# Exchanging two transpose copies between ScalarE and VectorE, and copying x out earlier, in the opening of a linear-attention + SwiGLU kernel

## Chip, cores, metric

One core of a Trainium2 chip. The metric is the device time of one execution in microseconds; lower is better. Most comparisons below use several executions of each kernel, taken in turn on the same chip. The four groups of experiments ran on four chips (0, 7, 6 and 9), so a kernel is compared with the kernel before of its own rounds; sums over all rounds mix chips.

## The reference, cut to what matters

For each of 8 batches and 8 heads, 576 tokens of 64 dimensions: softmax of the queries along the head dimension, softmax of the keys along the tokens, `kv = k^T v`, `x = q kv`. Then a SwiGLU block over all 4608 tokens (512 wide, 1536 hidden).

```python
q_s = exp(q - max) / sum          # along the 64 dimensions of a head
k_s = exp(k - max) / sum          # along the tokens
kv  = einsum('bhsd,bhse->bhde', k_s, v)
x   = einsum('bhsd,bhde->bhse', q_s, kv)   # -> [4608, 512]
out = (silu(x @ w_gate) * (x @ w_val)) @ w_out
```

Inputs and output are fp32; the kernel computes in bf16 with fp32 sums.

## The kernel before: the parts concerned

Heads come in two groups of four (group 0 and 1). A group's normalised queries `qs` are transposed on TensorE into PSUM (`tp`) in two pieces, of 5 and 4 token blocks (640 and 512 columns), and copied to SBUF as `qt`. `kv` is scaled into `kn`, and `x = kn^T qt` is copied into `xt`, which the gate and value products read. Only batch 0 has this opening; later batches hide behind the SwiGLU products.

```python
spin(8)                    # warm-up products on zeros
spin(6, first)             # ... from the first row sum of batch 0's queries on
key_sum(0)
turn_pe(0, 0, 0)           # transposes, group 0, piece of 640 and piece of 512
turn_pe(0, 0, 1)
turn_out(0, 0, 0, nc.scalar)     # copy PSUM -> SBUF
exp_of("k", 0, 1)
turn_out(0, 0, 1, nc.scalar)
norm_mul(0, 1, BANKS)
spin(6)
kv_first(0)                # the first kv product
key_sum(1)
scale_first(0, nc.scalar)  # kn of group 0, both halves on ScalarE
turn_pe(0, 1, 0)
turn_pe(0, 1, 1)
turn_out(0, 1, 0, nc.vector)
turn_out(0, 1, 1, nc.vector)
xp0 = x_mm(0, 0, 0), x_mm(0, 0, 1)      # the first x product
kv_first(1, *BANKS[0])     # the second kv product, values in two pieces
kv_first(1, *BANKS[1])
x_out(0, 0, 0, xp0[0], (nc.scalar, None))
scale_first(1, nc.vector)  # kn of group 1: half on ScalarE, half on VectorE
x_out(0, 0, 0, xp0[0], (None, nc.vector))
x_out(0, 0, 1, xp0[1])
xp1 = x_mm(0, 1, 0), x_mm(0, 1, 1)      # the second x product
...
for m in range(MT):
    m_unit(0, S, m, by_group=(m == 0))  # the gate and value products start
```

A later part turns out to matter, the preparation of batch 1 some 28 us further on:

```python
exp_of("q", 1, 0)
exp_of("q", 1, 1)
norm_sum(1, 0)
norm_mul(1, 0)             # VectorE, bf16, 128x1152
norm_sum(1, 1)
...
i = norm_mul(1, 1)
cast_v(1, 0)               # GpSimd: batch 1's values, fp32 -> bf16
c = cast_v(1, 1)
tc.add_manual_dep(c.ins, i.ins.name, SYNC, reason="order of the vector port")
```

The second cast is made to wait for the second normalisation; the first cast waits only for its data.

The softmax here doesn't subtract the row's maximum and nothing guards it: scores larger than these inputs give would overflow.

Of the kernel before, what the change touches and what calls it, by code (L numbers as in the profile page):

```python
# [15 lines left out]
def kernel(  # L16
# [10 lines left out]
    nc = tc.nc  # L27
# [19 lines left out]
    def bank(name):  # L47
        return psp.tile([128, 512], FP32, tag="ps", name=name)
# [57 lines left out]
    def copy(eng, out, in_):  # L106
        if eng is nc.scalar:
            nc.scalar.copy(out=out, in_=in_)  # L108
        else:
            eng.tensor_copy(out=out, in_=in_)  # L110
# [5 lines left out]
    def exp_of(what, b, G, pieces=((0, T),)):  # L116
        s = st.setdefault((b, G), {})
        e = s["e" + what] = at.tile([128, T, 2, 64], BF16, tag="e" + what, name="e" + what)
        src = raw[what, b, G].rearrange("p h (t d) -> p t h d", d=64)
        for t0, t1 in pieces:  # L120
            nc.scalar.activation(out=e[:, t0:t1], in_=src[:, t0:t1], func=AF.Exp)  # L121
# [21 lines left out]
    def norm_mul(b, G, pieces=((0, T),), engs=None):  # L143
        s = st[b, G]
        eq2 = s["eq"].rearrange("p t h d -> p (t h) d")
        qs = s["qs"] = at.tile([128, T, 128], BF16, tag="qs", name="qs")
        for (t0, t1), eng in zip(pieces, engs or (nc.vector, nc.vector)):
            n = 2 * (t1 - t0)
            last = eng.tensor_mul(  # L149
                qs[:, t0:t1, :].rearrange("p t (h d) -> p (t h) d", d=64),  # L150
                eq2[:, 2 * t0:2 * t1, :],
                s["rr"][:, 2 * t0:2 * t1].to_broadcast([128, n, 64]),
            )
        return last

    def turn_pe(b, G, i):
        s = st[b, G]
        if i == 0:
            s["qt"] = at.tile([128, T, 128], BF16, tag="qt", name="qt")
        t0, t1 = BANKS[i]  # L160
        tp = s["tp", i] = psp.tile([128, 1024], BF16, tag="ps", name="tp")
        for t in range(t0, t1):
            j = t - t0
            nc.tensor.transpose(  # L164
                out=tp[:, j * 128:(j + 1) * 128], in_=s["qs"][:, t, :], identity=ident
            )

    def turn_out(b, G, i, eng):
        s = st[b, G]
        t0, t1 = BANKS[i]  # L170
        copy(
            eng,
            s["qt"][:, t0:t1, :],
            s["tp", i][:, 0:(t1 - t0) * 128].rearrange("p (t c) -> p t c", c=128),
        )
# [19 lines left out]
    def x_mm(b, G, i):  # L195
        s = st[b, G]
        t0, t1 = BANKS[i]
        xp = [bank("xp") for _ in range(2)]
        for g in range(2):
            for h in range(2):  # L200
                r = slice(64 * h, 64 * h + 64)
                nc.tensor.matmul(  # L202
                    out=xp[h][64 * g:64 * g + 64, 0:64 * (t1 - t0)],
                    lhsT=s["kn"][r, g, :],
                    rhs=s["qt"][r, t0:t1, 64 * g:64 * g + 64],
                    start=True, stop=True,
                )
        return xp

    def x_out(b, G, i, xp, engs=(nc.scalar, nc.vector)):  # L210
        t0, t1 = BANKS[i]
        n = 64 * (t1 - t0)
        c0 = b * S + 64 * t0
        for h in (h for h in range(2) if engs[h] is not None):
            copy(engs[h], xt[:, 2 * G + h, c0:c0 + n], xp[h][:, 0:n])
# [137 lines left out]
    with tc.manual_schedule():  # L353
# [31 lines left out]
        def spin(n, after=None):  # L385
            idle = bank("idle")
            for _ in range(n):
                i = nc.tensor.matmul(out=idle, lhsT=zero[:, 0:128], rhs=zero, start=True, stop=True)  # L388
                if after is not None:
                    tc.add_manual_dep(i.ins, after.ins.name, SYNC, reason="start of the warm-up")  # L390
                    after = None
# [12 lines left out]
        def kv_first(G, t0=0, t1=T):  # L404
            s = st[0, G]
            if t0 == 0:
                s["kv"] = [bank("kv") for _ in range(2)]
            for t in range(t0, t1):
                for g in range(2):
                    for h in range(2):  # L410
                        nc.tensor.matmul(  # L411
                            out=s["kv"][g][HALF[h], 0:64], lhsT=s["ek"][HALF[g], t, h, :],
                            rhs=v16[G][HALF[g], h, 64 * t:64 * t + 64],
                            start=(t == 0), stop=(t == T - 1),
                        )

        def scale_first(G, eng1):
            s = st[0, G]
            kn = s["kn"] = at.tile([128, 2, 64], BF16, tag="kn1", name="kn1")
            nc.scalar.mul(kn[:, 0, :], s["kv"][0][:, 0:64], s["kvr"][:, 0:1])  # L420
            if eng1 is nc.scalar:
                nc.scalar.mul(kn[:, 1, :], s["kv"][1][:, 0:64], s["kvr"][:, 1:2])
            else:
                nc.vector.tensor_scalar_mul(kn[:, 1, :], s["kv"][1][:, 0:64], s["kvr"][:, 1:2])
# [5 lines left out]
        turn_pe(0, 0, 1)  # L430
        turn_out(0, 0, 0, nc.scalar)
        exp_of("k", 0, 1)
        turn_out(0, 0, 1, nc.scalar)
        norm_mul(0, 1, BANKS)
        spin(6)
        kv_first(0)
        key_sum(1)
        scale_first(0, nc.scalar)
        turn_pe(0, 1, 0)
        turn_pe(0, 1, 1)  # L440
        turn_out(0, 1, 0, nc.vector)
        turn_out(0, 1, 1, nc.vector)
        xp0 = x_mm(0, 0, 0), x_mm(0, 0, 1)
        kv_first(1, *BANKS[0])
        kv_first(1, *BANKS[1])
        x_out(0, 0, 0, xp0[0], (nc.scalar, None))
        scale_first(1, nc.vector)
        x_out(0, 0, 0, xp0[0], (None, nc.vector))
        x_out(0, 0, 1, xp0[1])
        xp1 = x_mm(0, 1, 0), x_mm(0, 1, 1)  # L450
        x_out(0, 1, 0, xp1[0])
# [153 lines left out]
```

## Time and profile before

| what | us |
|---|---|
| three runs | 311.02, 311.06, 311.29 |
| span of the profiled run | 309.7 (time 311.57) |
| first gate product starts | 14.22 |
| the second x product waits for the scaled kv | 0.42 |

The span is that of the profile, from first to last instruction; the time is 1.8 us longer. The prediction below shows the chain of the opening and the timeline of ScalarE and VectorE (in brackets idle time and what ended it). One more view was not read closely before predicting and is needed later: TensorE's own timeline from the beginning (start us, duration us, engine, line, instruction, count; in brackets idle time and what ended it).

```profile
1.22 3.60 PE L388 MATMUL idle<-zero 128*128 128x512 bf16 x8 [1.22 <-DVE sel L367]
6.23 2.74 PE L388 MATMUL idle<-zero 128*128 128x512 bf16 x6 [1.41 <-DVE rs L135]
9.97 1.56 PE L388 MATMUL idle<-zero 128*128 128x512 bf16 x6
11.46 0.48 PE L411 MATMUL kv<-v,ek 64*64 64x64 bf16 x36
```

The second batch of six warm-up products takes 2.74 us, the third, of six as well, 1.56 us. TensorE's clock stepped up meanwhile: the products start 0.43 us apart in the second batch and 0.22 us apart from 10.29 us on, and in the trace's record the clock is full from 10.2 us on, early in the third.

### The profile page before, as it was taken

To read this page: it belongs to the slowest core of one execution; us is meant where nothing else is said; L and a number is where in the kernel's file an instruction comes from. 1 tells how busy PE (TensorE), PEld (TensorE's weight loads), DVE (VectorE), ACT (ScalarE), POOL (GpSimd) and SP (SyncE) were. 2 spreads that over 40 slices of the span, in tenths; PEclk is the share of its full clock that TensorE was granted. 3 is DMA by queue.
4 is the path that set the end of the run, shared out by engine and by line. 5 is a ranking of instruction groups with operands and counts; after the bars stand their busy time and mean duration, and the time that the engine had idled before them with its cause. 6 is when DMAs were issued, how large, how long until landed. Compare 5 with 4: busy or idle time off the path is not lost.

```text
span 309.7 us, 5467 instructions
## 1 busy us (share of the span) xinstructions
PE 302.8 (98%) x2182; PEld 150.3 (49%) x2182; DVE 161.9 (52%) x286; ACT 146.3 (47%) x214; POOL 32.8 (11%) x39
## 2 busy tenths in 40 slices
PE   6999999999999999999999999999999999999995
PEld 2688745554445444454445444544444444444443
DVE  3844477945754566365826492639353324433421
ACT  5843578785674375547464737455043113312300
POOL 2960021510200110002000200000000000000000
PEclk9999999999999999999999999999999999999999
DMA  7999999999347815590739352605310302020133
GB/s 273 189 195 207 275 389 389 349 219 389 79 87 200 327 33 114 135 382 13 144 74 353 102 121 61 186 0 107 72 35 0 70 11 56 3 68 8 26 71 103
DMA packets 43018, 45.78 MB, mean 148 GB/s; under 512 B 19568, under 2 KB 28272, under 8 KB 42992
## 3 DMA queue, kind: packets, MB, share of 16 engines
q1 hardware_dynamic: 34096, 39.95, 43.4%
q0 software_dynamic: 8752, 5.31, 12.0%
q8 instruction: 17, 0.28, 0.4%
q10 hardware_dynamic: 144, 0.16, 0.2%
q14 instruction: 9, 0.07, 0.1%
HBM read 37.75 MB, written 9.44 MB: 152 GB/s over the span
## 4 chain that ended last, share of the span: by engine, by line
PE 96%; DMA 1%; DVE 0%; ACT 0%; issue 0%
PE g_ps L284 30%; PE u_ps L284 30%; PE o_ps L317 29%; PE kv L189 2%; PE xp L245 1%; PE idle L388 1%; DMA q<-in_q_dram 1%; PE tp L164 1%; PE o_ps L338 1%; DVE rs L135 0%; PE xp L202 0%; PE kv L411 0%; ACT eq L121 0%; ACT xt L259 0%; PE ks L397 0%; DVE o_sb L342 0%
## 5 line engine op out<-in xcount | busy, mean ns | idle before, releaser
L291 ACT ACTIVATE sg<-g_ps 128x512 bf16<-128x512 f32 (+2 forms) x120 | 64.7, 554 | 133.6 <-PE g_ps L284 120.5
L293 DVE TENSOR_TENSOR hr<-sg,u_ps 128x512 bf16<-128x512 bf16 (+3 forms) x120 | 72.5, 616 | 86.3 <-PE u_ps L284 80.7
L284 PE MATMUL g_ps<-xt,wg 128*128 128x512 bf16 (+2 forms) x480 | 111.4, 358 | 0.1
L284 PE MATMUL u_ps<-xt,wv 128*128 128x512 bf16 (+2 forms) x480 | 111.3, 358 | 0.0
L317 PE MATMUL o_ps<-wo,hr 128*128 128x512 bf16 x420 | 93.9, 379 | 0.0
L284 PEld LDWEIGHTS <-wv 128*128 128x128 bf16 x480 | 46.9, 98 | 46.4
L284 PEld LDWEIGHTS <-wg 128*128 128x128 bf16 x480 | 46.3, 98 | 45.5 <-issue 0.6
L317 PEld LDWEIGHTS <-hr 128*128 128x128 bf16 x420 | 40.9, 98 | 48.6
L110 DVE COPY o_sb<-o_ps 128x512 f32<-128x512 f32 x33 | 22.4, 680 | 39.0 <-PE o_ps L317 39.0
L124 POOL CAST vb<-v 128x1152 bf16<-128x1152 f32 x14 | 17.8, 1277 | 135.8 <-DMA v<-in_v_dram 106.6
L135 DVE TENSOR_REDUCE rs<-eq 128x18 f32<-128x1152 bf16 (+2 forms) x18 | 21.7, 1213 | 12.7 <-ACT eq L121 12.7
L149 DVE TENSOR_TENSOR qs<-eq,rr 128x1152 bf16<-128x1152 bf16 (+2 forms) x18 | 22.1, 1234 | 0.1
L121 ACT ACTIVATE eq<-q 128x1152 bf16<-128x1152 f32 (+2 forms) x18 | 18.3, 1051 | 4.1 <-DMA q<-in_q_dram 4.0
L121 ACT ACTIVATE ek<-k 128x1152 bf16<-128x1152 f32 (+2 forms) x17 | 17.9, 1101 | 0.5 <-DMA k<-in_k_dram 0.5
L291 ACT ACT_TABLE_LOAD x12 | 15.4, 1283 | 0.2
L121 ACT ACT_TABLE_LOAD x11 | 14.1, 1283 | 0.2
L388 PE MATMUL idle<-zero 128*128 128x512 bf16 x20 | 7.9, 560 | 2.6 <-DVE rs L135 1.4
L259 ACT CAST xt<-xp 128x512 bf16<-128x512 f32 x14 | 7.8, 586 | 4.5 <-PE xp L245 4.5
L260 DVE CAST xt<-xp 128x512 bf16<-128x512 f32 x14 | 9.0, 683 | 0.7 <-PE xp L245 0.7
L189 PEld LDWEIGHTS <-ek 64*64 64x64 bf16 x504 | 6.3, 107 | 1.7 <-ACT qt L108 0.4
L189 PE MATMUL kv<-vb,ek 64*64 64x65 bf16 x504 | 6.7, 194 | 0.0
L245 PE MATMUL xp<-qt,kn 64*64 64x512 bf16 (+1 forms) x112 | 6.7, 292 | 0.0
(44 smaller groups left out, 67.4 us busy)
## 6 DMA issues: line engine op xcount, KB each, us to landing
q<-in_q_dram SPq DMA_DIRECT2D x16, 576.0 KB, 5.4
out_dram<-o_sb SPq DMA_DIRECT2D x70, 128.0 KB, 2.3
k<-in_k_dram SPq DMA_DIRECT2D x12, 576.0 KB, 7.2
v<-in_v_dram SPq DMA_DIRECT2D x12, 576.0 KB, 9.1
wo<-in_moe_w_out_dram POOLq DMA_DIRECT2D x4, 384.0 KB, 15.4
k<-in_k_dram SPq DMA_DIRECT2D x4, 320.0 KB, 8.2
k<-in_k_dram SPq DMA_DIRECT2D x4, 256.0 KB, 8.1
v<-in_v_dram SPq DMA_DIRECT2D x2, 320.0 KB, 6.9
```

The lines of the kernel that those rows point to most:

```text
L110: eng.tensor_copy(out=out, in_=in_)
L121: nc.scalar.activation(out=e[:, t0:t1], in_=src[:, t0:t1], func=AF.Exp)
L124: return nc.gpsimd.tensor_copy(out=vbs[G][:, :, :, 0:64], in_=raw["v", b, G].rearrange("p h (t d) -> p t h d", d=64),)
L135: i = nc.vector.reduce_sum(out=rs[:, 2 * t0:2 * t1], in_=eq2[:, 2 * t0:2 * t1, :], axis=mybir.AxisListType.X)
L149: last = eng.tensor_mul(qs[:, t0:t1, :].rearrange("p t (h d) -> p (t h) d", d=64), eq2[:, 2 * t0:2 * t1, :], s["rr"][:, 2 * t0:2 * t1].to_ ...
L189: nc.tensor.matmul(out=kv[g][HALF[h], c:c + 65], lhsT=ek[HALF[g], t, h, :], rhs=vbs[G][HALF[g], t, h, :], start=(t == 0), stop=(t == T - 1),)
L245: nc.tensor.matmul(out=o[h][HALF[g], c:c + 64 * (t1 - t0)], lhsT=kn[HALF[h], g, G, :], rhs=qt[G][HALF[h], t0:t1, 64 * g:64 * g + 64], star ...
L284: nc.tensor.matmul(out=gu[a][i][:, 0:w_], lhsT=(wg, wv)[a][:, kk, ms], rhs=xt[:, kk, c:c + w_], start=(kk == 0), stop=(kk == KT - 1),)
L291: nc.scalar.activation(out=sg[:, 0:w_], in_=g_ps[:, 0:w_], func=AF.Silu)
L293: nc.vector.tensor_mul(hr[:, m, r:r + w1], sg[:, 0:w1], u_ps[:, 0:w1])
L317: nc.tensor.matmul(out=o_ps, lhsT=hr[:, m, r0:r0 + 128], rhs=wo[:, m, :], start=(m == 0), stop=(m == MT - 1),)
L388: i = nc.tensor.matmul(out=idle, lhsT=zero[:, 0:128], rhs=zero, start=True, stop=True)
```

## The change

The intent: give each engine the copy that comes when it is free. ScalarE gives up group 0's second copy, which stands just ahead of its first scaling, and takes group 1's first copy from VectorE. VectorE then has room to copy x out before it scales. No instruction is added or removed.

```diff
         turn_out(0, 0, 0, nc.scalar)
         exp_of("k", 0, 1)
-        turn_out(0, 0, 1, nc.scalar)
         norm_mul(0, 1, BANKS)
+        turn_out(0, 0, 1, nc.vector)
         spin(6)
...
-        turn_out(0, 1, 0, nc.vector)
+        turn_out(0, 1, 0, nc.scalar)
         turn_out(0, 1, 1, nc.vector)
...
-        x_out(0, 0, 0, xp0[0], (nc.scalar, None))
+        x_out(0, 0, 0, xp0[0])
         scale_first(1, nc.vector)
-        x_out(0, 0, 0, xp0[0], (None, nc.vector))
         x_out(0, 0, 1, xp0[1])
```

## The prediction

> **What bounds the kernel now.** I read the page's first part, then the chain of waits that ended last, narrowed to the first 30 us, then the timeline of the two engines that the change touches, in the same stretch.
>
> The page first, for the question of which engine a saved microsecond has to reach:
>
> ```profile
> PE 302.8 (98%) x2182; PEld 150.3 (49%) x2182; DVE 161.9 (52%) x286; ACT 146.3 (47%) x214; POOL 32.8 (11%) x39
> ```
>
> TensorE is busy 98% of a span of 309.7 us. ScalarE and VectorE are about half busy, so their work counts only where TensorE stands still for it. The change sits in the opening, which ends when the first gate product starts at 14.22 us; from there TensorE runs with almost no gap. So the question is by how much that start moves. Part of the chain before it (start us, duration us, what):
>
> ```profile
> 11.53 0.41 PE kv L411 x36
> 11.94 0.31 PE ks L397 x9
> 12.25 0.52 PE tp L164 x9
> 12.77 0.37 PE xp L202 x8
> 13.14 0.36 PE kv L411 x35
> 13.49 0.02 issue
> 13.52 0.30 DVE kn L424
> 13.81 0.03 issue
> 13.84 0.45 PE xp L202 x8
> ```
>
> From 11.53 to 13.49 every piece is TensorE's own, in program order: the first kv product, the key sums, the transposes of the second group of queries, the first x product, the second kv product. Then comes the only real stop: the second kv product must be scaled into kn before the second x product can start. "Waits" puts it down as 0.42 us before that product. Only what moves this scaling, or what follows it, can move the end.
>
> What the two other engines do around it (start us, duration us, engine, line, instruction), ScalarE first:
>
> ```profile
> 9.78 0.69 ACT L108 COPY qt<-tp 128x640 bf16<-128x640 bf16 x1 [0.59 <-PE tp L164]
> 10.37 1.17 ACT L121 ACTIVATE ek<-k 128x1152 bf16<-128x1152 f32 x1
> 11.44 0.58 ACT L108 COPY qt<-tp 128x512 bf16<-128x512 bf16 x1
> 11.98 0.31 ACT L420 ACTIVATE kn<-kv,kvr 128x64 bf16<-128x64 f32 x1
> 12.20 0.31 ACT L422 ACTIVATE kn<-kv,kvr 128x64 bf16<-128x64 f32 x1
> 13.07 0.42 ACT L108 CAST xt<-xp 128x320 bf16<-128x320 f32 x1 [0.57 <-PE xp L202]
> 13.47 0.31 ACT L420 ACTIVATE kn<-kv,kvr 128x64 bf16<-128x64 f32 x1
> ...
> 12.28 0.17 DVE L402 RECIPROCAL kvr<-ks 128x2 f32<-128x2 f32 x1 [0.41 <-PE ks L397]
> 12.59 0.82 DVE L110 COPY qt<-tp 128x640 bf16<-128x640 bf16 x2
> 13.52 0.28 DVE L424 TENSOR_SCALAR kn<-kv,kvr 128x64 bf16<-128x64 f32 x1
> 13.72 1.54 DVE L110 CAST xt<-xp 128x320 bf16<-128x320 f32 x4
> ```
>
> Three things are to be seen. ScalarE is free from 12.51 to 13.07, VectorE from 11.88 (end of its last normalisation) to 12.28: both have room beside the chain. The two halves of the critical kn run at once, one per engine, 13.47 to 13.78 and 13.52 to 13.80. And VectorE's first copy of x waits until after kn, at 13.72.
>
> [...] the single records are 0.49 and 0.41 us on VectorE, 0.69 and 0.58 on ScalarE. [...] The trace has the overlap: the copy of 9.78 would end at 10.47 and the next starts at 10.37, and kn follows kn after 0.22 of its 0.31. [...] The trace shows about 0.1 us at each change between 128*128 and 64*64 (the last transpose starts at 12.55, streams about 0.05, and the first x product starts at 12.70). It stays as it is: TensorE's order is the same in both programs.
>
> **The change, part by part.** Comparing the order of instructions of the two built programs: nothing is added or removed, the tiles and sizes are the same, and three things move.
>
> (1) The 512 copy of group 0 leaves ScalarE (11.44, 0.58 us) for VectorE, where it comes right after the last normalisation: it can start near 11.80 (normalisation ends 11.88, VectorE's neighbours overlap by 0.08) and ends near 12.21. The reciprocal behind it waits for the key sums until 12.28 as before. Who gains? ScalarE's first kn at 11.98; but that needs the kv product, which ends at 11.94, so it can gain 0.03 at most. And the x product that uses it starts at 12.70 [...]; kn is out at 12.51. Gain on the path: 0.
>
> (2) The 640 copy of group 1 leaves VectorE (12.59, 0.49 us) for ScalarE. The transposes are out at 12.59 as before, and it takes 0.69. The next ScalarE instruction, the copy of x, could start at 13.07; now it starts at 12.59 + 0.69 - 0.10 = 13.17, 0.10 later. It lasts 0.42, so the critical kn on ScalarE can start at 13.17 + 0.42 - 0.10 = 13.49 to 13.50 in place of 13.47. It was waiting for the kv product then, not for ScalarE (the copy at 13.07 left the engine near 13.40). So of the 0.10 only 0.02 to 0.03 reaches the path: kn ends near 13.81, and TensorE goes on 0.05 later, at 13.86 in place of 13.84.
>
> (3) On VectorE one copy of x (320 columns) now comes before kn. The group 1 copy of 512 starts once its transposes are out, 12.77 + 0.04 = 12.81, where it started at 12.99 before. Then the copy of x starts at 12.81 + 0.41 - 0.08 = 13.14 (its data are there at 13.07) and kn at 13.14 + 0.48 - 0.08 = 13.54, in place of 13.52. Cost: 0.02, beside the 0.02 of ScalarE and not on top of it. In return the copies of x end earlier: the first at 13.62 in place of 14.20, the second near 14.16 in place of 14.53. The gate products that need them start at 14.37 and 14.62 as single records, [...] at the same pace as later groups (0.15, 0.14, 0.11 between starts against 0.14, 0.14, 0.11). So at most 0.01 us was lost there, and that is all there is to win.
>
> Sum: +0.02 at the second x product, -0.01 behind it, 0 elsewhere: between 0 and +0.03 us. [...] I put +0.04 between these.
>
> [...] the change also alters which bank a tile gets. In both programs each of the tiles from the second x product on takes a bank that is read out before TensorE gets there; from the third gate product on the order is the same with other bank numbers.
>
> **Rivals.** (a) ScalarE becomes the bound: it gets the slower copy (0.69 for 0.58 before) just ahead of the critical kn. Its idle 0.57 us before 13.07 speaks against; a transpose that is out later[...] speaks for it. It makes +0.1, at the worst +0.2: 311.2 to 311.3. (b) The swap was worth making because VectorE's copies of x came too late: the chain gives the first gate group 0.60 us against 0.49 for those after it, which looks like 0.11 us to win. Against: the single starts show no stop[...]. If it were real: -0.1, 310.95. (c) The opening gets shorter, but meets the weights: the first slice of the value weights is issued at 9.37 and such a transfer lands after a median of 5.1 us, near 14.5, and is used at 14.72. So no more than some 0.2 us could be won at all before that wait took the place of the other. (d) A shift of a few hundredths is swallowed by a later wait. TensorE does stop at 46 and 51 us for VectorE and ScalarE (0.2 and 0.3 us), but those waits hang on work that starts with TensorE's own earlier results and move along with it; I expect no swallowing, and it would make the time 311.06.
>
> **Range and chances.** 311.06 + 0.04 = 311.1 us. The three runs of before spread over 0.27 us (311.02 to 311.29), so scatter is larger than the effect: with it and the rivals from -0.1 to +0.2 I take 310.8 to 311.5. Two per cent is 6.2 us; the whole opening from 11.5 to 14.2 us is shorter than half of that, so only something unseen could do it: 0.5% for faster, 1% for slower.
>
> **What would show it.** In the changed kernel's timeline: ScalarE's kn for group 0 still at 11.98; its 640 copy at 12.59 with 0.69; its copy of x near 13.17; its critical kn at 13.50 [...]; VectorE's copy of x at 13.14 and kn at 13.54; the second x product at 13.86 and the first gate product at 14.24, within 0.1. Wrong would be: a second x product before 13.80 (I would have missed what held kn), a stop of TensorE at the first x product (12.70), or a first gate product that starts more than 0.15 us from 14.22.

Of the single records, 0.49 and 0.41 us are VectorE's copies of 640 and 512 columns, 0.69 and 0.58 us ScalarE's. A start that waited came 0.04 us after the end that it waited for (the scaling ends at 13.80, the second x product starts at 13.84). A term is cut from the sum: the terms that stand came to 0 to +0.03 us; the cut one was a possible later start of the scaling behind a copy on ScalarE, of a size that no trace here shows. The author put +0.04 us between the sum without and with it, so 311.06 + 0.04 = 311.1 us.

## The result, and the profile after

| | before | changed |
|---|---|---|
| runs of the same rounds | 311.02, 311.29, 311.06, 312.51, 311.36, 311.94 | 311.33, 311.95, 311.70, 313.17, 311.85, 312.05 |
| median | 311.33 | 311.90 |
| ratio | | 1.0015 (0.9991 to 1.0040) |

Every run whose state is on record, here and below, is recorded as "fast". When this text calls a run "slow", it means over 312.3 us, a line that is explained at the end, and "quick" means the rest. A ratio is the mean time of one kernel's fast runs over that of the other's of the same rounds, so not quite the ratio of the medians quoted. The median of 311.9 lies outside the predicted 310.8 to 311.5: either the change costs half a microsecond that the prediction did not see, or the scatter had been sized wrongly.

The profiled run of the changed kernel was one of the quick ones (311.33 us, span 309.5 us), so it cannot show where time went. It shows two things that the prediction did not expect. The first is TensorE's timeline in the opening:

```profile
1.23 3.40 PE L388 MATMUL idle<-zero 128*128 128x512 bf16 x8 [1.23 <-DVE sel L367]
6.29 1.47 PE L388 MATMUL idle<-zero 128*128 128x512 bf16 x6 [1.67 <-DVE rs L135]
8.88 1.46 PE L388 MATMUL idle<-zero 128*128 128x512 bf16 x6
10.77 0.48 PE L411 MATMUL kv<-v,ek 64*64 64x64 bf16 x36 [0.43 <-DMA v<-in_v_dram]
12.27 0.44 PE L202 MATMUL xp<-qt,kn 64*64 64x320 bf16 x8
12.53 0.46 PE L411 MATMUL kv<-v,ek 64*64 64x64 bf16 x36
13.41 0.47 PE L202 MATMUL xp<-qt,kn 64*64 64x320 bf16 x8 [0.42 <-ACT kn L420]
13.81 0.66 PE L284 MATMUL g_ps<-xt,wg 128*128 128x320 bf16 x4
```

The second batch of six warm-up products took 1.47 us here, not 2.74: the trace's record of the clock has it full from 4.3 us on, not from 10.2. This part of the program is the same in both kernels. The key sums behind it came 1.2 us earlier (7.60, not 8.77). Waits for the values and for VectorE took most of that back: the first kv product came 0.7 us earlier (10.77, not 11.46), the first gate product 0.4 us (13.81, not 14.22). From the second kv product (12.53) to the second x product (13.41) it is 0.88 us, against 12.97 and 13.84, 0.87 us, before.

The second is where half of those 0.4 us went. The waits of the stretch from 44 or 45 to 47 us (who <- for whom: total us, times, longest), before:

```profile
PEld L164 <- DVE qs L149: 0.5, 1, 0.5
```

and after:

```profile
PEld L164 <- DVE qs L149: 0.7, 1, 0.7
PE tp L164 <- DVE qs L149: 0.2, 1, 0.2
```

TensorE arrived earlier at batch 1's transposes and waited 0.2 us longer there for VectorE's normalised queries. In this trace those hang on batch 1's queries, which landed at 38.73 us, and not on TensorE. The page's chain of waits says the same in one line. Before:

```profile
PE 96%; DMA 1%; DVE 0%; ACT 0%; issue 0%
```

After:

```profile
PE 84%; DMA 8%; POOL 4%; DVE 2%; ACT 1%; issue 0%; SPq 0%
```

The chain no longer runs back to the start through TensorE. It leaves it at this wait and goes through the loads (DMA, and GpSimd, which issues the weight loads). Spans: 309.74 before, 309.49 after, so 0.25 us of the 0.42 us were left.

ScalarE's timeline of the changed kernel, to be held against the prediction's lines of before:

```profile
11.29 0.31 ACT L420 ACTIVATE kn<-kv,kvr 128x64 bf16<-128x64 f32 x1 [0.45 <-PE kv L411]
11.50 0.31 ACT L422 ACTIVATE kn<-kv,kvr 128x64 bf16<-128x64 f32 x1
11.89 0.69 ACT L108 COPY qt<-tp 128x640 bf16<-128x640 bf16 x1
12.64 0.43 ACT L108 CAST xt<-xp 128x320 bf16<-128x320 f32 x1
13.04 0.31 ACT L420 ACTIVATE kn<-kv,kvr 128x64 bf16<-128x64 f32 x1
```

Between its exponential and its first scaling ScalarE now sits idle for 0.45 us, waiting for TensorE: the freed room is not used. And in this run the 640 copy at 11.89 is out of the way before the copy of x can start, so it delays nothing.

### The profile page after: what moved, and what is told of

The parts are those of the page before. It is cut to its first block, busy times and chain, and to the rows that moved or that the text cites. A ratio compares the mean times of both kernels' runs of the same rounds, so it can differ in the third digit from the quotient of the medians.

```text
span 309.5 us, 5467 instructions
## 1 busy us (share of the span) xinstructions
PE 301.4 (97%) x2182; PEld 149.7 (48%) x2182; DVE 161.5 (52%) x286; ACT 146.5 (47%) x214; POOL 33.0 (11%) x39
## 4 chain that ended last, share of the span: by engine, by line
PE 84%; DMA 8%; POOL 4%; DVE 2%; ACT 1%; issue 0%; SPq 0%
PE o_ps L317 27%; PE g_ps L284 27%; PE u_ps L284 26%; DMA wo<-in_moe_w_out_dram 4%; DMA q<-in_q_dram 2%; PE kv L189 2%; DMA k<-in_k_dram 2%; POOL wg L96 1%; POOL wv L96 1%; PE xp L245 1%; DVE qs L149 1%; DVE rs L135 1%; PE o_ps L338 1%; POOL v L361 0%; ACT eq L121 0%; POOL v L358 0%
## 5 line engine op out<-in xcount | busy, mean ns | idle before, releaser
L121 ACT ACTIVATE eq<-q 128x1152 bf16<-128x1152 f32 (+2 forms) x18 | 18.3, 1053 | 4.2 <-DMA q<-in_q_dram 4.1
L121 ACT ACTIVATE ek<-k 128x1152 bf16<-128x1152 f32 (+2 forms) x17 | 18.0, 1103 | 0.8 <-DMA k<-in_k_dram 0.7
L388 PE MATMUL idle<-zero 128*128 128x512 bf16 x20 | 6.3, 471 | 2.9 <-DVE rs L135 1.7
```

The costliest lines, as they stand in the source:

```text
L121: nc.scalar.activation(out=e[:, t0:t1], in_=src[:, t0:t1], func=AF.Exp)
```

## The experiments

Three questions. Does the change have a cost of its own (theory B) or is it lost in scatter (theory A)? Where does the scatter come from? Can it be taken away, so that the two kernels can be compared without it?

### e1 to e4: both kernels again, and each part alone

e1 is the kernel before, unaltered; e2 the changed kernel, unaltered.

> The kernel before, unaltered, timed against itself. Theory A (the change is worth nothing that can be seen; the medians of 311.33 and 311.9 us differ by scatter from outside the program): the runs of this one kernel spread over 0.5 us or more and its ratio to itself is as far from 1 as 0.1 per cent. Theory B (the change costs a real 0.4 to 0.5 us): this kernel against itself stays within 0.05 per cent. Its trace shows which of two openings it had: full TensorE clock from about 10 us (idle products 0.43 us apart until then, first gate product at 14.2) or from about 4 us (0.22 us apart, first gate product at 13.8).

> The changed kernel again. Theory A: ratio 0.999 to 1.001, and the same two openings as the kernel before; from the last matmul of the second kv product to the second x product 0.61 us in either, as both traces so far have it. Theory B: ratio 1.0013 to 1.002, so 0.4 to 0.6 us.

e3 has the exchange of copies without the earlier copy of x (against the kernel before):

```diff
-        turn_out(0, 0, 1, nc.scalar)
         norm_mul(0, 1, BANKS)
+        turn_out(0, 0, 1, nc.vector)
-        turn_out(0, 1, 0, nc.vector)
+        turn_out(0, 1, 0, nc.scalar)
```

> The two copies of the queries exchanged, the copy of x left behind the scaling on VectorE. Theory A: ratio 0.999 to 1.001; the second x product 0.61 us after the last matmul of the second kv product. Theory B, if the exchange of copies carries the cost: ratio 1.0013 to 1.002; if the copy of x carries it: 1.000.

e4 has the earlier copy of x without the exchange:

```diff
-        x_out(0, 0, 0, xp0[0], (nc.scalar, None))
+        x_out(0, 0, 0, xp0[0])
         scale_first(1, nc.vector)
-        x_out(0, 0, 0, xp0[0], (None, nc.vector))
```

> The copy of x moved ahead of the scaling on VectorE, the copies of the queries as before. VectorE's last copy of queries ends at 13.41 in the trace of before, so the copy of x starts near 13.33, ends the engine's turn near 13.73, and the scaling starts there in place of 13.52: the second x product 0.2 us later (0.8 us after the last kv matmul). Theory A expects a ratio of 1.0003 to 1.0010 for this one, from these 0.2 us alone; theory B, if the copy of x carries the cost, 1.0013 to 1.002.

Measured, with the kernel before at 311.25 to 312.84 in 11 runs of the same rounds (mean 311.65):

| | range | mean | ratio (95%) |
|---|---|---|---|
| e1, before again | 311.25 to 312.37 | 311.59 | 0.9998 (0.9981 to 1.0016) |
| e2, changed again | 311.31 to 312.85 | 312.12 | 1.0015 (0.9997 to 1.0034) |
| e3, copies only | 311.49 to 312.55 | 311.78 | 1.0004 (0.9988 to 1.0021) |
| e4, copy of x only | 311.47 to 313.06 | 312.05 | 1.0016 (0.9996 to 1.0035) |

The kernel before spreads over 1.6 us in these rounds, six times the 0.27 us of its first three runs. But the changed kernel's mean is 0.47 us over it, as in the first rounds (0.48), so theory B was not out. The expectations are split too: the spread of e1 (1.1 us) is what theory A asked for, its ratio to itself (0.9998) what theory B asked for, and the ratios of e2 and e4 lie in theory B's range.

The traces decide what the change does on the path. e3 had the late clock step, as before, and its values in time. It is therefore the clean test of the prediction's step on ScalarE. Its ScalarE timeline:

```profile
12.59 0.69 ACT L108 COPY qt<-tp 128x640 bf16<-128x640 bf16 x1
13.18 0.43 ACT L108 CAST xt<-xp 128x320 bf16<-128x320 f32 x1
13.50 0.33 ACT L420 ACTIVATE kn<-kv,kvr 128x64 bf16<-128x64 f32 x1
```

The prediction had 12.59, 13.17 and 13.50. From the last matmul of the second kv product to the second x product it is 0.64 us in the single records of e3 and 0.61 in before and e1: the exchange costs 0.03 us, no more. In e2 and e4 the second piece of group 1's values came late and TensorE waited for it inside the second kv product. The chain of e2 in the opening (start us, duration us, what):

```profile
7.98 5.56 DMA v<-in_v_dram
13.54 0.04 issue
13.58 0.37 PE kv L411 x16
13.96 0.30 ACT kn L420
14.26 0.04 issue
14.30 0.45 PE xp L202 x8
```

So e4 could not show the 0.2 us that I expected of the copy of x alone: its kv product was held up so long that VectorE was done with the copy (at 13.51) before the scaling could start (13.68), and from kv to x it is 0.60 us. The lateness does not need the change. The transfer was issued at 8.0 us; up to about 11.4 us e2 has the same instruction order as before, and e4 up to 13.0 us, when its piece (landed at 13.24) was nearly in. And e11 below, whose opening is that of the kernel before, had the piece as late (13.21).

Then the slow runs. The profiled runs of e1 (312.37 us) and e2 (312.85 us) were slow ones, and both lost time in the same place, near 42 us, where VectorE normalises batch 1's first queries and GpSimd casts its first values. VectorE and GpSimd in that stretch, before (a quick run):

```profile
41.84 1.36 DVE L149 TENSOR_TENSOR qs<-eq,rr 128x1152 bf16<-128x1152 bf16 x1
...
42.20 2.01 POOL L124 CAST vb<-v 128x1152 bf16<-128x1152 f32 x1 [20.27 <-DMA v<-in_v_dram]
46.22 1.15 POOL L124 CAST vb<-v 128x1152 bf16<-128x1152 f32 x1 [2.01 <-DVE qs L149]
```

e2 (a slow run):

```profile
42.23 2.26 DVE L149 TENSOR_TENSOR qs<-eq,rr 128x1152 bf16<-128x1152 bf16 x1
...
42.14 1.14 POOL L124 CAST vb<-v 128x1152 bf16<-128x1152 f32 x1 [20.27 <-DMA v<-in_v_dram]
```

The same two instructions, 1.36 and 1.14 us alone, but whichever starts second is stretched: before, the cast, to 2.01; in e2, the normalisation, to 2.26. The normalisation that started at 42.23 ended at 44.49, which is 1.21 us after the cast's end at 43.28; so of its 1.36 us it had done about 0.15 in the 1.05 us beside the cast, if the rest ran at its own speed (my estimate). In e1 it is the same: the cast ran from 41.70 to 42.84, and the normalisation from 42.04 to 44.05, again 1.21 us after the cast's end. It holds in the other direction too: in the seven in which the normalisation started first, the cast ended 1.00 or 1.01 us after it, wherever it had started. The held-up casts cost nothing that can be seen (the seven traced runs that had one took 311.03 to 311.66 us). A held-up normalisation delays batch 1's transposes, for which TensorE then waits (0.6 us in e1 and e2).

The sign of it was in the page of before: the group of casts has a mean of 1277 ns in 14 instructions, while the one at 46.22 took 1.15 us. (Two more of the 14, at 55 and 59 us, were stretched too.)

### e5 to e8: the race at 42 us taken out, reversed, and a longer warm-up

e5 is the kernel before, and e6 the changed kernel, with the first cast ordered behind the first normalisation:

```diff
-        norm_mul(1, 0)
+        i0 = norm_mul(1, 0)
...
-        cast_v(1, 0)
+        c = cast_v(1, 0)
+        tc.add_manual_dep(c.ins, i0.ins.name, SYNC, reason="order of the vector port")
         c = cast_v(1, 1)
```

> The kernel before, with GpSimd's cast of batch 1's first values made to wait for VectorE's normalisation of batch 1's first queries. In the traces so far the one of these two that starts first runs at full speed and holds the other up: where the cast won (41.70 before 42.04, 42.14 before 42.23), the normalisation took 2.0 to 2.3 us in place of 1.36 and TensorE waited some 0.5 us for it at 47 us. Theory C (the slow runs of both kernels are those in which the cast wins): no run over 312.2, ratio to before 0.9985 to 0.9997, normalisation always 1.36. Rival (the slow runs come from somewhere else): the same spread as before, 311.2 to 312.8, ratio 0.9995 to 1.0005.

> The changed kernel with the same order of cast and normalisation. Theory A plus C: the same time as e5 within 0.15 us (mean of the runs), so the change itself is worth nothing and only its runs that lost the race were longer. Theory B (the change has a cost of its own of 0.4 to 0.5 us): e6 stays 0.4 us above e5.

e7 forces the opposite order, on the kernel before:

```diff
-        norm_mul(1, 0)
+        c0 = cast_v(1, 0)
+        i0 = norm_mul(1, 0)
+        tc.add_manual_dep(i0.ins, c0.ins.name, SYNC, reason="cast first")
...
-        cast_v(1, 0)
```

> The kernel before with the opposite order: the normalisation waits until the cast has ended, in every run. Theory C: the cast ends near 43.3 and the normalisation near 44.6 in place of 43.2, so 1.0 to 1.4 us more, of which the first 0.2 to 0.5 fall into slack: ratio 1.002 to 1.004, all runs over 312. Rival: less than 0.3 us more, 1.001 or under.

e8 is e5 with a longer warm-up:

```diff
-        spin(8)
+        spin(12)
         spin(6, first)
```

> e5 with 12 warm-up products in place of 8 before the first sum, so that TensorE has work up to 6.3 us. So far its full clock came at 4.3 us in one trace and at 9.4 to 10.6 in five; I expect 8 or earlier now in every run, the first gate product near 13.8 in place of 14.2 to 14.5, and half of it kept behind the wait at 46 us: 0.2 to 0.4 us under e5, ratio 0.998 to 0.999. Rival (the values, which land at 12 to 13 us, then hold TensorE instead): the first gate product at 14.0 or later and no more than 0.1 us under e5.

Measured; the kernel before in these rounds: 311.21 to 312.61, mean 311.89, 11 runs.

| | range | mean | ratio (95%) |
|---|---|---|---|
| e5, before, ordered | 311.20 to 311.75 | 311.49 | 0.9987 (0.9972 to 1.0001) |
| e6, changed, ordered | 311.03 to 312.18 | 311.54 | 0.9988 (0.9970 to 1.0006) |
| e7, cast first | 312.82 to 314.10 | 313.33 | 1.0046 (1.0029 to 1.0062) |
| e8, ordered, longer warm-up | 310.95 to 311.86 | 311.44 | 0.9985 (0.9970 to 1.0001) |

VectorE and GpSimd in e5:

```profile
42.11 1.36 DVE L149 TENSOR_TENSOR qs<-eq,rr 128x1152 bf16<-128x1152 bf16 x1
...
43.54 1.14 POOL L124 CAST vb<-v 128x1152 bf16<-128x1152 f32 x1 [21.75 <-DVE qs L149]
```

and in e7:

```profile
43.43 1.36 DVE L149 TENSOR_TENSOR qs<-eq,rr 128x1152 bf16<-128x1152 bf16 x1 [1.70 <-POOL vb L124]
...
42.26 1.14 POOL L124 CAST vb<-v 128x1152 bf16<-128x1152 f32 x1 [20.29 <-DMA v<-in_v_dram]
```

With the order fixed both instructions run at full speed and the slow runs are gone, in both kernels. With it reversed every run is slow; 1.44 us over the kernel before, a little more than expected (ratio 1.0046, not 1.002 to 1.004). And e6 equals e5 within 0.05 us, while the unordered pair differed by 0.47: theory A and C, against B.

The kept traces show how much of the scatter passes through this place. I take the time of each traced run and subtract the time at which this normalisation ended: 311.57 - 43.20 = 268.37 us before, 312.85 - 44.49 = 268.36 in e2, 313.17 - 44.79 = 268.38 in e7. In all sixteen traces of this document, of both kernels and of every variant, the rest is 268.27 to 268.40 us, while the times go from 311.03 to 313.17. So whatever made one traced run longer than another, but for about 0.1 us, had happened when that normalisation ended, at 43 to 45 us.

e8 put the clock step where I expected it (6.9 us) but brought nothing (0.05 us under e5, not 0.2 to 0.4; first gate product 14.31). In its trace TensorE waited 0.8 us for the first values, and the chain went through VectorE's normalisation of group 1, whose queries had landed at 8.40 us (7.92 before). My rival was right: in this trace a warm TensorE only waits for the loads.

### e9 to e12: the four kernels once more

e9 is the kernel before, e10 the changed one, e11 is e5 again, e12 is e6 again, all unedited, to double the runs.

> The kernel before against itself once more, as the measure for the next three. Mean 311.5 to 311.9, with one or two runs over 312.3.

> The changed kernel once more. Twelve runs of it so far average 312.06, 33 of the kernel before 311.7. Theory A: this falls back towards the kernel before, within 0.2 us of the mean of all runs of before in this call. Theory B: a third time 0.4 to 0.5 us above.

> e5 again. Theory C: mean 0.2 to 0.5 us under the kernel before, no run over 312.2. Rival (the gain in e5 was scatter): the mean of before within 0.1 us.

> e6 again. Theory A plus C: within 0.15 us of e11, and with e5 and e6 together within 0.1 us. Theory B: 0.4 us above e11. In its trace the second x product comes 0.64 us after the last matmul of the second kv product where the values landed in time (0.61 in e11), 0.60 where they were late: 0.03 us is what the change costs on the path.

| | range | mean | ratio (95%) |
|---|---|---|---|
| before, same rounds | 310.98 to 312.21 | 311.55 | |
| e9, before | 310.91 to 311.47 | 311.31 | 0.9990 (0.9977 to 1.0003) |
| e10, changed | 311.03 to 313.77 | 311.73 | 1.0004 (0.9980 to 1.0027) |
| e11, before, ordered | 311.23 to 312.07 | 311.52 | 0.9997 (0.9985 to 1.0009) |
| e12, changed, ordered | 311.08 to 311.82 | 311.43 | 0.9994 (0.9982 to 1.0006) |

Five of e10's six runs lie at 311.03 to 311.57, one at 313.77. The third time there is no difference of 0.4 us: e10's mean is 0.18 over that of before, through its one run of 313.77. For e9 I had expected a mean of 311.5 to 311.9 and one or two slow runs; it had 311.31 and none. e11 did not repeat e5's gain of 0.4 us: here the kernel before had no run over 312.3 to lose. The trace of e12 has 0.64 us from the last kv matmul to the second x product, as expected; e11's 0.60 was one of the late values, so the 0.61 to hold against it is that of before, e1 and e9.

### e13 and e14: does a later opening lose the race more often?

The last way in which the change could cost more than its 0.03 us: if a shift of hundredths made the lost race more frequent. Both kernels get two more idle products ahead of the first kv product, e13 the kernel before, e14 e5:

```diff
         norm_mul(0, 1, BANKS)
-        spin(6)
+        spin(8)
         kv_first(0)
```

> The kernel before with two more idle products (0.43 us) ahead of the first kv product, so that the opening ends later by a known time. Theory D (the later the opening ends, the oftener GpSimd's cast starts before VectorE's normalisation at 42 us and costs another 0.5 us or more): most runs over 312.3, mean 0.7 to 1.1 us above the kernel before, and in the trace the cast ahead of a normalisation of 2.0 us or more. Rival (the outcome at 42 us does not hang on the opening): 0.2 to 0.45 us above, as for e14 against its own base, and one run in ten over 312.3.

> e5 with the same two idle products: the delay without the race. Both theories: mean 311.5 plus 0.3 to 0.45, so 311.8 to 311.95, and spread as narrow as in e5 (no run over 312.6). So e13 minus e14 is the price of the lost races: 0.3 us or more under theory D, under 0.15 for the rival.

Measured, with before at 311.09 to 312.78 (mean 311.76): e13 311.09 to 312.59, mean 311.56, ratio 0.9998 (0.9978 to 1.0017); e14 311.29 to 311.93, mean 311.52, ratio 0.9996 (0.9981 to 1.0010). Theory D got no support: e13 minus e14 is 0.04 us, and one run of e13 in six was over 312.3. My sum for e14 failed too: a delay of 0.43 us was expected to cost 0.3 and cost nothing. TensorE's timeline of e13 tells why, for the profiled run at least:

```profile
8.86 1.89 PE L388 MATMUL idle<-zero 128*128 128x512 bf16 x8
10.74 0.48 PE L411 MATMUL kv<-v,ek 64*64 64x64 bf16 x36
```

The clock was full early (4.9 us), so the eight idle products took 1.89 us and ended where the values landed anyway (10.70 us; compare 10.77 for the kv product in the trace of the changed kernel). The race was won in this trace. So the test did not delay the opening in the run that we can look into (first gate product 13.79), and how much it did in the others is unknown. Theory D was hardly tested.

The traces at hand say more than this test. Here are the nine without a fixed order, sorted by the first gate product (us):

| trace | first gate product | normalisation starts | cast starts |
|---|---|---|---|
| e10, changed | 13.79 | 41.34 | 42.32 |
| e13, before, later | 13.79 | 41.69 | 42.10 |
| changed | 13.81 | 41.64 | 42.10 |
| e9, before | 14.12 | 41.67 | 42.30 |
| before | 14.22 | 41.84 | 42.20 |
| e3, copies only | 14.25 | 41.80 | 42.17 |
| e4, copy of x only | 14.39 | 41.94 | 42.13 |
| e1, before | 14.49 | 42.04 | 41.70 |
| e2, changed | 14.68 | 42.23 | 42.14 |

The two lost races are those with the two latest openings. The start of the normalisation follows the opening: in six of the nine it comes 27.55 us after the first gate product. What ties them together stands in the chain of e2: a SwiGLU activation (`sg`) that needs a gate product, then the load of the exponential's table (L121), then the exponential of batch 1's queries.

```profile
37.66 0.38 ACT sg L291
38.04 0.02 issue
38.05 1.28 ACT L121
39.34 0.01 issue
39.35 1.17 ACT eq L121
40.52 0.02 issue
40.55 1.36 DVE rs L135
```

The cast waits for its own load and starts anywhere from 41.70 (e1, the earliest) to 42.32. So a late opening brings the normalisation into the reach of the cast, and theory D's order of things is in these traces. That it makes lost races more frequent is not shown: nine traces are few, and they were sorted after the fact. For the change it matters little: 0.03 us later can turn only a race whose two starts lie that close, and none of the nine does (the closest differ by 0.09).

### All runs together

| kernel | runs | mean | median | over 312.3 |
|---|---|---|---|---|
| before | 60 | 311.65 | 311.57 | 7 |
| changed | 18 | 311.95 | 311.75 | 5 |
| before, ordered (e5, e11) | 11 | 311.50 | 311.51 | 0 |
| changed, ordered (e6, e12) | 11 | 311.49 | 311.41 | 0 |

The line at 312.3 was drawn after the fact, in the gap between the quick and the slow traces. Of the nine traces without a fixed order, the two in which the cast started first are of runs of 312.37 and 312.85 us; the seven in which the normalisation started first are of runs of 311.03 to 311.66. Of the 34 runs with the cast behind the normalisation (e5, e6, e8, e11, e12, e14) none is over 312.3; of the 95 with neither order fixed 16 are. In the same rounds as those 34, 6 of 50 are; that 0 and 6 differ by chance has a probability of about 1 in 25, and of 0 and 16 about 1 in 200, for a line drawn after the fact. The two traced slow runs are lost races, a loss that is forced (e7) makes every run slow, and without the race none is: that is why I take the slow runs for lost races. That each untraced one is such a race was not seen. The granted clock does not set them apart: it was 0.994 to 1.000 in slow runs, and two quick runs had 0.994 as well (311.48, 311.71).

The ordered version is the better one to keep. It is not clearly faster in the middle (medians 311.51 and 311.57), but it has no slow runs.

## Why the prediction was wrong, point by point

**The mechanism on the path was right.** The prediction said that the first scaling gains nothing from the copy taken off ScalarE: e3 and the trace after show ScalarE idle there, waiting for TensorE. It said that the copy of 640 pushes ScalarE's copy of x to 13.17 and the critical scaling to 13.50: e3 has 13.18 and 13.50. It said +0.02 at the second x product: e3, e6 and e12 have 0.03 where the clock step was late and the values came in time; where they were late, or the clock step early, there is 0.01 at most. The VectorE half of the sum came true as well. In e12 the last kv matmul is 0.22 us earlier than before (13.01, not 13.23), and VectorE's copy of x and its scaling start at 12.92 and 13.32: shifted back, 13.14 and 13.54, the two figures predicted. The term that is cut from the sum, a later start of the scaling behind a copy, did not come: the scaling starts 0.32 us after the start of a copy of 0.43 (e3), 0.11 us before its end, so nothing is added there. What a scaling takes beyond a copy is inside its own 0.31 us, which the sum already held: ScalarE's copies of 640, 512 and 320 columns take 0.69, 0.58 and 0.42 us, from which I estimate 0.20 us for 64. Rival (b) is out: the earlier copies of x gained nothing behind the second x product (0.37 us from it to the first gate product in e6 and e12 with them, 0.37 in e3 without; 0.38 in e4 with them alone, 0.38 before). And with the race removed the means of the two kernels differ by 0.01 us (11 runs each, 95% interval about 0.28 either way): that excludes theory B's 0.4 to 0.5, while the 0.03 itself is seen only as a distance in traces.

**The step that failed is "311.06 + 0.04" with its scatter.** The prediction took 311.06, the median of three runs, for the level of the kernel before, and their spread of 0.27 us for its scatter, and built 310.8 to 311.5 on both. In 60 runs the kernel before has a median of 311.57, 0.5 us higher, and spreads over 1.9 us (310.91 to 312.84). The added 0.04 was right, the term that it was added to was not: the kernel before itself lies outside that range. If six of its 60 runs are drawn at random, their median exceeds 311.5 in two draws of three; 311.9 or more comes in one of twenty. So the three runs were a lucky draw (only 12 of the 60 are at 311.29 or below), and the 311.9 of the changed kernel an unlucky one, or its slow runs are more frequent (see below).

**What the scatter is made of.** Three things scatter, and the first hangs in part on the other two. (1) The race at 42 us: lost, it stretched the normalisation by 0.65 us (e1) and 0.90 us (e2); the stretched cast stood in the trace. The profile of before could have shown it; I had not asked which instructions of GpSimd fall on VectorE's. (2) The clock step: full clock came between 4.3 and 5.4 us in four traces and between 9.1 and 10.6 in eleven (6.9 in e8, with its longer warm-up), and with it the first gate product at 13.8 to 14.05 or at 13.9 to 14.7. The trace's record of the clock (in the packed trace; no view above prints it) has the stretch at full clock 300.37 us long before and 303.79 us after, 3.41 us apart, and it has one of these two lengths in all sixteen traces. In the kernel before the warm-up pauses from 4.8 to 6.2 us; what decides whether the step comes early or late was not shown. (3) The loads: the second piece of group 1's values, 128 KB, landed between 12.43 and 13.54 us in sixteen traces, with the ends of its issue within 0.15 us of each other. Where the opening was early, TensorE met them, or the weights: in e5 and e12 it waited 0.4 us at 16.5 us for a slice of gate weights. Rival (c) had foreseen that, for the value weights.

**Rival (d) was half right.** The prediction said that the waits at 46 and 51 us "hang on work that starts with TensorE's own earlier results and move along with it". For the wait at 46 this holds in thirteen of the sixteen traces: there the exponential of batch 1's queries follows directly on the table load, which follows TensorE's gate products. In three (before, changed, e14) the queries landed after that load was done, and the exponential waited for them. In the changed kernel's trace this was 0.29 us, and it swallowed half of the 0.4 us that TensorE had won. So a gain in the opening can be lost to the queries' landing, while a delay beyond it is passed on. What the rival lacked besides is the wait of VectorE for GpSimd.

**What stays open.** The unordered changed kernel averages 0.30 us above the kernel before (18 and 60 runs), because 5 of 18 runs were slow against 7 of 60; the quick ones alone average 311.55 and 311.52. That can be chance (a difference this large comes about once in ten if both lose equally often). It was not settled whether the change makes late openings, and with them lost races, more frequent. The slowest runs (313.17 and 313.77, so 1.6 and 2.2 us over the median of before) were not traced; in the traces a lost race stretched the normalisation by at most 0.90 us and, ending 1.21 us after the cast, could do so by about 1.0 us (1.14 + 1.21 - 1.36, my estimate), so a late opening or something else was added there.

## What to carry to other kernels

Before sizing a range, look for instructions in the trace that are longer than their twins: here a cast of 2.01 us beside others of 1.15 was a race that about a microsecond hung on in the runs that lost it. Then ask whether the path runs there: in e8 VectorE lost the same race to later casts twice (normalisations of 2.25 us at 54.2 and 2.31 at 59.5), TensorE did not wait, and the run took 311.53 us. If such a normalisation and a cast meet and one of them is on the path, order them by hand; here that cost nothing (mean of 11 runs ordered 311.50 us, of 60 before 311.65), as the cast had slack. And a change worth hundredths in an opening that waits by turns for a clock, for loads and for itself cannot be judged by medians of six runs: compare the distance between two events on the path, in traces of the same kind.
